# A recurrent cell followed by an MLP: the first group's instructions in a new order, with SyncE's queue and the PSUM banks written out, and a transposition of two steps at once

## The chip, the cores and the metric

The kernel runs on one core of one Trainium2 chip. The metric is the device time of one execution in microseconds (us). Engines are named as in the profile: PE is TensorE, PEld its weight load, DVE is VectorE, ACT is ScalarE, POOL is GpSimd, and SP is SyncE, which here does nothing but issue DMAs.

## The reference, cut to what matters

For each of 32 pairs of batch and head (4 by 8) a recurrence runs over 768 positions with vectors of 40 (abridged):

```python
m_new = np.maximum(f_gate[:, :, t] + m, i_gate[:, :, t])
f_stab = np.exp(f_gate[:, :, t] + m - m_new); i_stab = np.exp(i_gate[:, :, t] - m_new)
C = f_stab * C + i_stab * np.einsum('bhd,bhe->bhde', vt, kt)
n = f_stab * n + i_stab * kt
h = np.einsum('bhde,bhe->bhd', C, qt)
h = C @ qt;  nq = n @ qt          # per batch and head
y[:, :, t] = sigmoid(o_gate[:, :, t]) * h / np.maximum(np.abs(nq), 1.0)
```

The result, arranged as 3072 tokens of 320 numbers, goes through `h = x @ w_in` (320 by 2048), `g = maximum(0.01 h, h)` and `g @ w_out` (2048 by 320). The two weight matrices arrive as 64-bit floats.

## The kernel before, in words

**Steps, chunks and groups.** The 768 positions are cut into six chunks of 128. A *step* is one chunk of one batch, with its eight heads: steps 0 to 3 are chunk 0, steps 4 to 7 chunk 1, and so on. A *group* is the 512 tokens of one chunk in all four batches, and the MLP runs a group at a time. Groups 1 to 5 follow a plan by unit numbers (VISITS, MIXES and so on) which the change leaves alone. The first group is another matter: while its MLP runs, chunk 1 is computed, the weights are still arriving and are brought to 32 bits. Its work is listed by hand in a long string, ORDER, which `first_chunk` reads from left to right and turns into calls. The string fixes the order of the instructions on TensorE, DVE, ACT and POOL (a manual schedule). SyncE's queue is not among them: the tile scheduler places its DMAs.

**Chunk 0** is computed with plain attention. In ORDER, `g`, `ge` and `ug` are the gates of a chunk (`gates` L289, two scans and small operations on DVE; `gates_exp` L319; `gates_T` L341, their transposes on TensorE). `mk` and `ab` (`mask_first` L455, `spread_first` L462) spread them over TensorE, and `exp` (`exp_first`, L475) takes the exponential of two heads on ACT, four times a step. `tr` (`u_transpose`, L584) transposes k and q, `tc` copies the result to SBUF as kqT on ACT or DVE, `sc` (`u_scores`, L599) multiplies q and k, `scm` (`scores_mix`, L610, two per step, DVE) multiplies scores with the exponentials, `val` (`u_values`, L680) multiplies with v, `st` (`state`, L615) and `stc` (L626) make the state behind the chunk, `den` and `gate` (L692) finish the step on DVE, `o` is its output gate on ACT. `x` (`u_x`, L881) transposes the step's result, and `xc` (L890) copies it as xT for the MLP.

**Chunk 1** is computed in halves of 64 positions. `us` (`u_split`, L566) transposes k and q of a step in four quadrants of TensorE, `qs` scales q by its gate, `tq` (`split_qs`, L557) transposes the scaled q of one step, `ex` are the exponentials (L500 on ACT), two heads at a time after a mask on POOL (`pm`, L492), `up` (`u_parts`, L647) makes the scores and the states of the halves, `upl` (`u_plain`, L715) the values, `ux` the transposes of the result, `ug2` the gates of the chunk after it. `fd` loads a step (`load`, L361, and `spread`), `ll` are later loads, `lw` loads a weight tile (L207).

**The MLP of group 0** is 32 units (`ff`, `ff_units` L911). ff 0 to ff 15 each multiply x by two blocks of w_in in products of 256 columns, 20 matmuls at L918, and ACT applies the leaky ReLU (L926). ff 16 to ff 31 multiply by w_out (L953). Units of later groups use L918 with 512 columns.

**Weights.** `narrow_weights` (`nw`, L251) turns a tile of 64-bit weights into 32 bits: one ACT operation (L263) and six on DVE (L265 to L280), which ORDER interleaves one by one with other work. Tiles 0 to 3 are w_in (1280 columns, in two loads each) and tiles 4 to 11 are w_out (640). ff 0, 4, 8 and 12 are the first to need tiles 0, 1, 2 and 3; ff 16 + 4m is the first to need tiles 4 + 2m and 5 + 2m.

**PSUM.** Eight banks: the MLP's products use four (pool `psf`), everything else of the cell the other four (pool `psc`, one tag with four buffers). With the rotating buffers, the fifth allocation waits until the readers of the first are done, in program order.

**Gate inputs.** f and i of chunk 0 (f0 and i0) are each loaded four times, into four groups of 32 partitions, f0 through ACT's queue and i0 through SP's (L93, L94). ACT's queue also issues the gate loads of chunks 1 and 2 (`load_fi`).

Of the kernel before, what the change touches and what calls it, by code (L numbers as in the profile page):

```python
# [22 lines left out]
def kernel(  # L23
# [68 lines left out]
    for r in range(RG):  # L92
        nc.scalar.dma_start(f0[ts(r, BH), :], f_all[:, :P])  # L93
        nc.sync.dma_start(i0[ts(r, BH), :], i_all[:, :P])  # L94
# [266 lines left out]
    def load(s, i=None):  # L361
# [13 lines left out]
        flat = w[:].rearrange("p h t -> p (h t)")
        d["w"] = flat[:, : H * SL].rearrange("p (h t) -> p h t", t=SL)
        if c == 1:
            for u in range(2):
                for i in range(2):
                    nc.sync.dma_start(  # L380
# [57 lines left out]
    def spread(s):  # L438
# [3 lines left out]
        for u in range(2):  # L442
            nc.sync.dma_start(d["w"][ts(u, SL)], a_dr[c, 0, u, b * H : (b + 1) * H, :].partition_broadcast(SL))

    def spread_q(s):
# [111 lines left out]
    def split_qs(s):  # L557

        tq = [psc.tile([P, H, SL], F32, name=f"tq{u}", tag="c") for u in range(2)]
        for h in range(H):  # L560
            for u, toks, rows in subs(s):
                nc.tensor.matmul(tq[u][rows, h, :], lhsT=st[s]["qs"][toks, h], rhs=ident[toks, toks], start=True, stop=True)
# [722 lines left out]
```

## Time and profile before

| what | value |
|---|---|
| three runs, us | 492.03, 491.97, 485.73 |
| median, us | 491.97 |
| time of the profiled execution, us | 488.21 |
| its span, us | 486.4 |
| PE busy in the span | 98% |
| DVE busy | 73% |
| ACT busy | 40% |
| POOL busy | 33% |

The profiled execution is one run of the program with the profiler on. Its span runs from the first to the last recorded instruction, and the execution's own time is 1.8 us more. A row with times in us gives first the start, counted from the start of the span, then the length, then the engine and the instruction with its line. In a row by groups, the number behind the bar is the busy time, then the mean of one instruction in ns, then the idle time of the engine just before the group and what ended it. In a row by windows come the window, its length, then the busy times (with the numbers of instructions) of PE, PE's weight loads, DVE, ACT and POOL, and at the end the granted clock of TensorE as a share of full speed, the mean busy share of the 16 DMA engines and their GB/s.

### The profile page before, as it was taken

What the parts mean: (1) busy time and instruction counts of PE and PEld (TensorE: products, weight loads), DVE (VectorE), ACT (ScalarE), POOL (GpSimd) and SP (SyncE); (2) the same over time, 40 slices, a digit from 0 to 9 for tenths busy, and PEclk for the clock granted to TensorE, in tenths of its full rate; (3) what the DMA queues carried; (4) which work ended last, traced back from release to release, by engine and by line L of the source; (5) the groups of instructions that cost most, each with busy time, mean ns of one, the idle gap of its engine ahead of it and who ended that gap; (6) DMA issues with size and microseconds to landing.
All of it is one profiled execution on the core that took longest, in us unless ns stands there. A gap on an engine that the chain in (4) does not pass through costs nothing.

```text
span 486.4 us, 12790 instructions
## 1 busy us (share of the span) xinstructions
PE 476.2 (98%) x5145; PEld 378.6 (78%) x5145; DVE 357.5 (73%) x581; ACT 194.8 (40%) x509; POOL 158.6 (33%) x207
## 2 busy tenths in 40 slices
PE   8899999899999999999999999999999999999997
PEld 7788887677746489965559985558998899988997
DVE  3887788978926999677898878679899968335611
ACT  3766549554442240414251131425024642156310
POOL 4074342443401816636370654544210002000020
PEclk9979999999999999999999999999999999999999
DMA  8999878775545577776776767754151030100001
GB/s 147 194 206 164 210 180 207 166 167 114 143 138 100 143 158 215 170 179 162 156 190 183 173 156 185 192 135 139 43 230 42 1 108 1 42 16 1 0 1 55
DMA packets 142187, 63.41 MB, mean 130 GB/s; under 512 B 110320, under 2 KB 130352, under 8 KB 142128
## 3 DMA queue, kind: packets, MB, share of 16 engines
q1 hardware_dynamic: 141744, 62.47, 54.3%
q8 instruction: 40, 0.66, 0.5%
q10 hardware_dynamic: 384, 0.13, 0.1%
q14 instruction: 19, 0.16, 0.1%
HBM read 51.68 MB, written 8.27 MB: 123 GB/s over the span
## 4 chain that ended last, share of the span: by engine, by line
PE 90%; DVE 3%; ACT 3%; issue 1%; POOL 1%; POOLq 0%; DVEq 0%
PE po L994 32%; PE ph L918 28%; PE ph L844 8%; PE po L953 5%; PE pe L844 4%; PE pT L754 3%; PE sd L661 3%; PE warm L339 1%; PE pa L684 1%; PE sd L666 1%; ACT w L483 1%; DVE qn L671 1%; PE hN L724 1%; PE tk L576 1%; ACT kqT L582 1%
## 5 line engine op out<-in xcount | busy, mean ns | idle before, releaser
L918 PE MATMUL ph<-xT,w_in 64*128 64x512 f32 (+1 forms) x800 | 144.0, 513 | 0.1
L918 PEld LDWEIGHTS ph<-xT,w_in 64*128 64x128 f32 x800 | 77.9, 190 | 56.7 <-issue 51.3
L994 PE MATMUL po<-w_out,acts 128*128 128x160 f32 x640 | 91.0, 301 | 0.0
L994 PEld LDWEIGHTS po<-w_out,acts 128*128 128x128 f32 x640 | 87.5, 190 | 3.4 <-ACT w L500 1.5
L926 ACT ACTIVATE acts<-ph 128x512 f32<-128x512 f32 (+1 forms) x80 | 37.4, 508 | 89.6 <-PE ph L918 89.1
L641 POOL TENSOR_TENSOR S<-S,f 40x336 f32<-40x336 f32 x36 | 32.5, 903 | 83.4 <-PE pT L754 53.1
L500 ACT ACTIVATE w<-w,gT 128x64 f32<-128x64 f32 x160 | 41.7, 339 | 27.8 <-POOL w L492 27.8
L994 PE MATMUL po<-raw,acts 128*128 128x160 f32 x320 | 45.1, 300 | 0.0
L994 PEld LDWEIGHTS po<-raw,acts 128*128 128x128 f32 x320 | 44.0, 190 | 0.0
L1027 POOL TENSOR_TENSOR y<-y,raw 128x160 f32<-128x160 f32 x10 | 5.5, 555 | 112.0 <-ACT y L1026 112.0
L671 DVE TENSOR_TENSOR qn<-w,sd 64x512 f32<-64x512 f32 x40 | 27.3, 683 | 18.6 <-PE sd L666 12.1
L953 PE MATMUL po<-w_out,acts 128*128 128x320 f32 x128 | 38.2, 454 | 0.0
L866 DVE SCALAR_TENSOR_TENSOR acts<-ph,acts 128x512 f32<-128x512 f32 x32 | 20.6, 685 | 20.6 <-ACT acts L864 20.6
L492 POOL TENSOR_TENSOR w<-w,i 128x512 f32<-128x512 f32 x20 | 32.8, 1644 | 6.9 <-DMA w<-a_dr 3.6
L553 DVE TENSOR_TENSOR qn<-kqT,late 64x512 f32<-64x512 f32 x32 | 34.0, 1062 | 1.0
L953 PEld LDWEIGHTS po<-w_out,acts 128*128 128x128 f32 x128 | 24.7, 198 | 10.0 <-issue 1.2
L768 POOL TENSOR_TENSOR xb<-xb,den 128x320 f32<-128x320 f32 x16 | 11.6, 727 | 48.9 <-DVE xb L765 48.9
L864 ACT ACTIVATE acts<-pe 128x512 f32<-128x512 f32 x32 | 17.4, 594 | 19.1 <-PE pe L844 19.0
L772 DVE STREAM_TRANSPOSE x<-xb 128x512 f32<-128x512 f32 x16 | 17.7, 1107 | 8.0 <-POOL xb L768 8.0
L661 PEld LDWEIGHTS sd<-kqT 40*64 40x64 f32 x640 | 19.6, 135 | 4.6 <-issue 4.2
L870 ACT ACTIVATE acts<-acts 128x512 f32<-128x512 f32 x32 | 19.7, 633 | 8.0 <-DVE acts L866 8.0
L994 PE MATMUL po<-raw 128*128 128x160 f32 x160 | 22.7, 300 | 0.0
(171 smaller groups left out, 768.0 us busy)
## 6 DMA issues: line engine op xcount, KB each, us to landing
w<-a_dr SPq DMA_DIRECT2D x40, 128.0 KB, 3.6
rb<-in_k_dram SPq DMA_DIRECT2D x64, 80.0 KB, 2.7
rb<-in_q_dram SPq DMA_DIRECT2D x64, 80.0 KB, 2.5
rb<-in_o_gate_dram SPq DMA_DIRECT2D x64, 80.0 KB, 2.4
xT<-x_dr SPq DMA_DIRECT2D x32, 160.0 KB, 3.2
late<-a_dr SPq DMA_DIRECT2D x32, 128.0 KB, 3.2
x_dr<-x SPq DMA_DIRECT2D x16, 256.0 KB, 2.8
kn<-in_k_dram SPq DMA_DIRECT2D x24, 160.0 KB, 4.1
```

The lines of the kernel that those rows point to most:

```text
L492: nc.gpsimd.tensor_tensor(w, w, cm2.unsqueeze(1).to_broadcast([P, H, SL]), op=ALU.add)
L500: yield nc.scalar.activation(w[:, h, :], w[:, h, :], AF.Exp, bias=gT[c][:, 0, bh : bh + 1], scale=1.0)
L553: nc.vector.tensor_tensor(mixed(s)[rows, 1 - r], d["kqT"][rows, 1].rearrange("p (h t) -> p h t", t=SL), d["ea"][rows], op=ALU.mult,)
L641: nc.gpsimd.tensor_tensor(new, old, g, op=ALU.mult)
L661: nc.tensor.matmul(bank[1 - u][toks, h, :], lhsT=kqT[rows, 0, ts(h, SL)], rhs=kqT[rows, 1, ts(h, SL)], start=True, stop=True,)
L671: nc.vector.tensor_tensor(mixed(s)[toks, u], w[toks], bank[1 - u][toks], op=ALU.mult)
L844: nc.tensor.matmul(ph[r][:], lhsT=parts["w", key][n][part, at : at + P], rhs=xs[key][part, slot, :], start=start and slot == 0, stop=stop ...
L866: nc.vector.scalar_tensor_tensor(fs[r], in0=ph[r][:], scalar=1.0 + EPS, in1=fs[r], op0=ALU.mult, op1=ALU.add,)
L918: nc.tensor.matmul(ph[r][:, cols], lhsT=w_row(r, slot, j), rhs=xT[DP * r : DP * (r + 1), slot, bs, :], start=(slot == 0), stop=(slot == KC ...
L926: nc.scalar.activation(acts[:, f, cols], ph[r][:, cols], AF.Prelu, alpha=0.01)
L953: nc.tensor.matmul(po[n][:], lhsT=acts[:, f, ts(n, P)], rhs=w_out[:, f, :], start=(f == 0), stop=(f == NF - 1),)
L994: nc.tensor.matmul(bank[:], lhsT=left[:, f, :], rhs=right[:, f, :], start=f == 0, stop=f == KH - 1)
```

## The change

The change does five things, all in the first group.

1. ORDER is written anew. TensorE's pieces of chunk 0 come in another sequence (`sc 0` and `sc 1` back to back, `val` 0 to 3 spread among transposes, scores and states; `x 2` and `st 3` behind ff 0), `us 7` and the `tq` of step 5 stand ahead of ff 16, and the `nw` steps of DVE come in another interleaving.
2. SyncE's queue is in the manual schedule too, so that every load goes out in the order of the string. The loads, `fd` above all, are cut into pieces with names of their own (`fk` for k, `fv` for v, `fs` for the spread gates, `lv` for a w_out tile), and the loads of f0 and i0 (`mf`, `mi`), the memsets (`zk`, `zs`, `zr`), the identities (`id`, `ib`) and the mask (`cm`) become entries of the string as well. The last argument of a load chooses the queue: 1 is ACT's, 0 is SP's. The i0 pieces are now the second, fifth, seventh and ninth DMA of SP; ACT's queue issues only the four of f0.
3. The four buffers of `psc` become four tags of one buffer, and a string of 59 digits, BANKS, says for each allocation of the first group which bank it gets.
4. `split_qs` transposes the scaled q of two steps, s and s + 1, in four quadrants of TensorE; ORDER calls it for steps 4 and 6 in place of four calls for 4, 5, 6 and 7.
5. Behind the first group the PSUM pool is closed, and a pool with four rotating buffers opens in its place for the rest.

The diff, cut to its core (the replacements of `nc.sync` by `queue(on)` and of `psc.tile` by `bank_of` go on in the same way in the other functions):

```diff
-    psc = ctx.enter_context(tc.tile_pool(name="psc", bufs=4, space=PSUM))
+    banks_stack = ctx.enter_context(ExitStack())
+    psc = banks_stack.enter_context(tc.tile_pool(name="psc", bufs=1, space=PSUM))
...
+    banks = []
+    later = []
+
+    def bank_of(shape, name):
+
+        if later:
+            return later[0].tile(shape, F32, name=name, tag="c")
+        return psc.tile(shape, F32, name=name, tag=f"c{banks.pop(0)}")
...
-    for r in range(RG):
-        nc.scalar.dma_start(f0[ts(r, BH), :], f_all[:, :P])
-        nc.sync.dma_start(i0[ts(r, BH), :], i_all[:, :P])
...
+    def queue(on):
+        return nc.scalar if on else nc.sync
+
+    def load_f0(r, on):
+        queue(on).dma_start(f0[ts(r, BH), :], f_all[:, :P])
+
+    def load_i0(r, on):
+        queue(on).dma_start(i0[ts(r, BH), :], i_all[:, :P])
...
+    def load_fi(c, on=0):
         t = fi[c] = wk.tile([BH, 2, P], F32, name="fi")
-        eng = nc.scalar if c < 3 else nc.sync
+        eng = queue(on)
         eng.dma_start(t[:, 0, :], f_all[:, ts(c, P)])
         eng.dma_start(t[:, 1, :], i_all[:, ts(c, P)])
 
-    load_fi(1)
-    load_fi(2)
...
-        tg = psc.tile([P, 5, BH], F32, name="tg", tag="c")
+        tg = bank_of([P, 5, BH], "tg")
...
     def split_qs(s):
 
-        tq = [psc.tile([P, H, SL], F32, name=f"tq{u}", tag="c") for u in range(2)]
+        tq = [bank_of([P, H, SL], f"tq{u}") for u in range(2)]
+        at = [(n, u, toks, rows, rows if n == 0 else slice(SL * u, SL * u + D)) for n in range(2) for u, toks, rows in subs(s)]
         for h in range(H):
-            for u, toks, rows in subs(s):
-                nc.tensor.matmul(tq[u][rows, h, :], lhsT=st[s]["qs"][toks, h], rhs=ident[toks, toks], start=True, stop=True)
-        for u, toks, rows in subs(s):
-            nc.scalar.copy(mixed(s)[rows, u], tq[u][rows])
+            for n, u, toks, rows, to in at:
+                nc.tensor.matmul(tq[u][to, h, :], lhsT=st[s + n]["qs"][toks, h], rhs=ident[toks, toks], start=True, stop=True)
+        for n, u, toks, rows, to in at:
+            nc.scalar.copy(mixed(s + n)[rows, u], tq[u][to])
...
+    BANKS = "01230123030210321031231031021020201320131231012012302320312"
     ORDER = """
-warm 12; g 0; ld 0 0; mk 0; ab 0; ge 0; ld 0 1; ld 1 0; lo 1; ld 0 2; ld 1 1; ld 2 0; ug 0; exp 0 0
-ld 1 2; exp 1 0; exp 1 2; exp 0 2; exp 0 3; tr 0 0; tc 0 0 0; tr 0 1; exp 0 1; tr 1 0; tc 0 1 0
-exp 1 3; ld 2 1; tr 1 1; sc 0; lw 0 0; scm 0 0; lw 0 1; tc 1 0 0; scm 0 1; mk 2; ab 2; lo 0; tc 1 1 0
-ld 3 0; g 1; ld 3 1; ld 3 2; sc 1; exp 1 1; scm 1 1; ld 2 2; exp 2 0; tr 2 0; tr 2 1; tc 2 1 0; lw 1 0
-lw 1 1; vu 0; exp 2 2; val 0; fi 3; exp 3 0; lo 2; exp 3 2; st 0; scm 1 0; stc 0 0 0; exp 2 3
-stc 0 1 0; den 0; exp 2 1; lo 3; tc 2 0 1; sc 2; o 1; lw 2 0; o 0; scm 2 0; gate 0; gp 0; ge 1
-scm 2 1; nw 0; val 1; den 1; x 0; xc 0 1; gate 1; tr 3 0; tr 3 1; tc 3 1 1; nw 0; nw 0; gp 1; x 1
-tc 3 0 0; sc 3; xc 1 1; vu 3; nw 0; nw 0; st 3; vu 2; vu 1; val 2; exp 3 1; exp 3 3; stc 3 1 1; st 2
-stc 2 1 1; scm 3 1; scm 3 0; val 3; nw 0; tiles; ps 3; stc 2 0 1; stc 3 0 1; nw 0; o 2; den 2; den 3
-gate 2; o 3; gate 3; nw 1; st 1; nw 1; nw 1; ug 1; ff 0; gp 2; x 2; xc 2 1; gp 3; nw 1; nw 1; x 3
-xc 3 1; ff 1; nw 1; ff 2; nw 1; ps 0; g 2; lw 2 1; nw 2; ff 3; lw 3 0; lw 3 1; ps 2; ff 4; ff 5; nw 2
-nw 2; ff 6; nw 2; ff 7; fd 4; lw 4; lw 5; stc 1 0 1; ps 1; vu 4; nw 2; nw 2; nw 2; nw 3; nw 3; nw 3
-nw 3; nw 3; nw 3; nw 3; nw 4; ff 8; ff 9; ff 10; nw 4; ff 11; ff 12; nw 4; nw 4; ff 13; nw 4; nw 4
-nw 4; stc 1 1 0; pm 4; sn 4 0; fd 5; ll 5 1; nw 5; ll 4 1; us 4; lw 6; lw 7; fd 6; lz 6; vu 6; fd 7
-qs 5; qs 4; pm 6; us 5; lw 8; nw 5; nw 5; nw 5; nw 5; nw 5; ff 14; pm 5; nw 5; ll 5 2; lw 9; nw 6
-nw 6; lz 7; nw 6; lz 4; ex 4 3; nw 6; ff 15; ll 6 0; ex 4 3; ex 4 2; nw 6; ll 4 2; nw 6; ge 2; nw 6
-pm 7; nw 7; ex 6 3; ex 6 3; tq 4; sn 5 0; nw 7; ll 7 0; ll 7 1; vu 5; up 4; nw 7; ff 16; ff 17; ex 7 3
-ff 18; ff 19; nw 7; ll 8 0; nw 7; nw 7; nw 7; nw 8; nw 8; nw 8; nw 8; ug2 2; nw 8; nw 8; tq 5; upl 4
-lw 10; nw 8; vu 7; ll 6 1; nw 9; nw 9; nw 9; lw 11; lz 5; fd 8; ex 7 3; nw 9; ll 9 0; nw 9; ex 5 3
-nw 9; sn 6 0; nw 9; ex 5 3; ff 20; nw 10; nw 10; qs 6; ex 5 2; up 5; us 7; qs 7; nw 10; nw 10; ff 21
-sn 7 0; ff 22; ux 4; upl 5; ll 9 1; nw 10; nw 10; nw 10; nw 11; nw 11; nw 11; ex 6 2; ff 23; pv 8
-sq 9; nw 11; ll 7 2; nw 11; tq 7; us 6; ll 8 1; pm 8; lz 8; ex 8 3; tq 6; ff 24; nw 11; nw 11; xb0
-ll 6 2; up 6; ex 7 2; up 7; ff 25; upl 6; fd 9; sn 9 0; upl 7; kq 9; fd 10; pv 9; sq 8; ll 8 2; pm 9
-kq 8; ll 11 1; sq 11; fd 11; ll 10 1; sn 8 0; ll 9 2; ex 8 3; ll 11 0; lz 9; vu 8; vu 9; ff 26; ff 27
-ff 28; ff 29; ux 5; ux 6; ux 7; sq 10; ff 30; ex 8 2; ff 31; ex 9 3; ex 9 3; ll 10 0; ex 9 2
+mf 3 1; ld 0 2 0; mi 1 0; mf 2 1; id; ld 0 0 0; cm; ld 1 1 0; mi 2 0; ib; ld 0 1 0; zk 1; mi 3 0
+mf 1 1; ld 1 0 0; mi 0 0; zr; warm 12; mf 0 1; zk 0; mk 0; zk 2; zk 3; lw 0 0 0; lw 0 1 0; zs 2; zs 3
+g 0; ge 0; ug 0; ab 0; exp 0 0; exp 1 0; exp 0 2; tiles; zs 1; ld 1 2 0; tr 0 0; tc 0 0 0; tr 0 1
+tr 1 0; tr 1 1; tc 1 1 1; tc 0 1 0; sc 0; exp 1 2; exp 1 3; fi 1 0; exp 1 1; tc 1 0 0; sc 1; scm 1 0
+scm 1 1; exp 0 3; mk 2; exp 0 1; scm 0 1; nw 0; scm 0 0; ld 2 0 0; lo 0 0; ab 2; zs 0; vu 0; g 1; o 0
+val 0; nw 0; nw 0; tr 2 0; ld 2 1 0; tr 2 1; nw 0; exp 3 0; exp 3 1; exp 2 0; exp 2 3; lo 1 0; val 1
+den 0; ld 3 0 0; tr 3 0; tc 2 0 1; gate 0; o 1; tc 2 1 1; lo 3 0; gp 0; sc 2; exp 2 1; ld 3 1 0; den 1
+tc 3 0 1; gate 1; gp 1; vu 1; tr 3 1; exp 2 2; scm 2 0; ps 0; x 0; scm 2 1; nw 0; tc 3 1 1; ld 2 2 0
+vu 2; ld 3 2 0; exp 3 2; sc 3; lw 1 0 0; exp 3 3; scm 3 0; scm 3 1; lo 2 0; vu 3; val 2; ge 1; x 1
+st 0; val 3; st 2; nw 0; ps 2; xc 0 1; lw 1 1 0; xc 1 1; nw 0; fi 2 0; o 3; st 1; stc 1 0 0; gate 3
+stc 0 1 1; fk 4 0; stc 0 0 1; o 2; den 3; gp 3; gate 2; ff 0; den 2; lw 2 0 0; gp 2; lw 2 1 0
+stc 1 1 1; ll 4 1 0; ug 1; fs 4 0; x 3; lw 3 0 0; lw 3 1 0; st 3; stc 3 0 1; xc 3 0; ll 6 0 0; fk 7 0
+lz 7; nw 1; nw 1; nw 1; nw 1; nw 1; pm 4; x 2; nw 1; nw 1; xc 2 1; vu 4; fk 5 0; lz 5; fs 5 0; ff 1
+ff 2; ff 3; nw 2; nw 2; nw 2; lz 4; nw 2; nw 2; stc 3 1 0; lv 5 0; nw 2; nw 2; lv 4 0; ll 5 1 0; us 4
+stc 2 0 1; fk 6 0; stc 2 1 0; ff 4; ff 5; ff 6; ff 7; nw 3; nw 3; nw 3; nw 3; nw 3; nw 3; ll 4 2 0
+fs 7 0; ff 8; nw 3; qs 4; ps 1; ff 9; ff 10; ex 4 3; qs 5; vu 6; nw 4; lv 6 0; nw 5; nw 5; ll 6 1 0
+ff 11; ps 3; pm 5; lv 7 0; nw 5; tq 4; lv 8 0; us 5; fv 4 0; ff 12; ll 7 1 0; nw 5; ex 4 2; fv 5 0
+ll 5 2 0; sn 4 0; nw 5; nw 5; fs 6 0; fv 6 0; ll 7 0 0; nw 4; ff 13; g 2; ff 14; sn 7 0; lv 9 0; lz 6
+nw 5; nw 4; nw 4; nw 4; nw 4; nw 4; nw 6; nw 6; nw 6; fi 3 0; ge 2; sq 9 0; fk 8 0; nw 6; ex 4 3
+ff 15; up 4; us 7; lz 8; nw 6; sn 5 0; ex 5 3; ex 5 3; ff 16; nw 6; lv 11 0; nw 6; sn 6 0; qs 7; nw 7
+nw 7; nw 7; vu 5; fk 9 0; nw 7; nw 7; lz 9; lv 10 0; ff 17; ff 18; nw 7; nw 7; ex 5 2; upl 4; ff 19
+pm 6; nw 9; nw 9; nw 9; ll 6 2 0; pm 7; ex 6 2; nw 9; nw 9; up 5; nw 9; nw 8; us 6; fk 10 0; nw 8
+ex 6 3; nw 8; nw 8; nw 8; ll 8 0 0; ff 20; ff 21; ux 4; upl 5; ll 7 2 0; ex 6 3; vu 7; nw 9; ff 22
+nw 8; nw 8; ll 9 1 0; fv 7 0; nw 10; sq 8 0; qs 6; ll 8 1 0; fs 9 0; ff 23; up 6; nw 10; nw 10; nw 10
+nw 10; nw 10; ex 7 3; tq 6; ff 24; ll 9 0 0; nw 10; ff 25; nw 11; ux 5; xb0; ug2 2; sn 9 0; fs 8 0
+upl 6; ll 8 2 0; ex 7 3; ex 7 2; up 7; fv 8 0; ff 26; ff 27; fv 10 0; ux 6; nw 11; nw 11; nw 11; nw 11
+nw 11; fk 11 0; fv 9 0; fs 11 0; pm 9; nw 11; upl 7; ll 9 2 0; ff 28; ff 29; ex 9 2; kq 8; ll 10 0 0
+ff 30; ux 7; fv 11 0; ff 31; vu 8; ex 9 3; ex 9 3; vu 9; sq 10 0; pv 9; pv 8; sn 8 0; pm 8; ex 8 3
+kq 9; ll 11 0 0; ex 8 3; fs 10 0; ll 10 1 0; ex 8 2; ll 11 1 0; sq 11 0
...
+        banks.extend(map(int, BANKS))
...
-            "warmer": warmer, "idle": idle, "fd": feed, "ll": load_late,
+            "warmer": warmer, "idle": idle, "fk": lambda s, on: load(s, 0, on), "fv": lambda s, on: load(s, 1, on), "fs": spread, "ll": load_late,
...
     with tc.manual_schedule(engines={E.PE, E.DVE, E.Activation, E.Pool}):
-        first_chunk()
+        with tc.manual_schedule(engines={E.SP}):
+            first_chunk()
+        banks_stack.close()
+        later.append(ctx.enter_context(tc.tile_pool(name="psl", bufs=4, space=PSUM)))
```

More of the change, by code (lines that the diff above doesn't have):

```diff
@@ L570, in u_split @@
         src = (d["k"], natural(s, 1))
-        bank = [psc.tile([P, H, SL], F32, name=f"tk{r}", tag="c") for r in range(2)]
+        bank = [bank_of([P, H, SL], f"tk{r}") for r in range(2)]
         for h in range(H):
@@ L601, in u_scores @@
         kqT = d["kqT"]
-        sc = d["sc"] = [psc.tile([P, PR, P], F32, name=f"sc{r}", tag="c") for r in range(2)]
+        sc = d["sc"] = [bank_of([P, PR, P], f"sc{r}") for r in range(2)]
         for j in range(PR):
@@ L651, in u_parts @@
         run(lazy.pop(s))
-        bank = [psc.tile([P, H, SL], F32, name=f"sd{r}", tag="c") for r in range(2)]
+        bank = [bank_of([P, H, SL], f"sd{r}") for r in range(2)]
         ends = 2 if c + 1 < NB else 1
@@ L859, in third @@
             def third():
[L860 removed]
+                pe.extend(bank_of([P, GT], f"pe{r}") for r in range(2))
                 rows(j, pe, "dif", True, True)
```

95 lines of the change are left out of this document (51 added, 44 removed).

## The prediction

> **What bounds the kernel now.** I read the page's busy shares first, then the stages, then the chain of work that ended last, in order of time.
>
> ```profile
> PE 476.2 (98%) x5145; PEld 378.6 (78%) x5145; DVE 357.5 (73%) x581; ACT 194.8 (40%) x509; POOL 158.6 (33%) x207
> ```
>
> ```profile
> 9.68 3.98 ACT w L483 x15
> ...
> 15.44 1.09 PE sc L606 x16
> ...
> 17.56 1.90 PE pa L684 x16
> ...
> 35.32 3.84 PE ph L918 x20
> ...
> 69.27 1.97 PE tk L576 x128
> ...
> 88.70 1.14 PE hN L724 x32
> ...
> 93.93 1.72 issue
> ...
> 102.37 0.22 PE xt L887 x2
> ...
> 106.11 0.96 PE tq L562 x30
> ...
> 111.89 0.17 PE sd L661
> ...
> 113.81 0.20 PE sd L666
> ...
> 119.07 8.81 PE po L953 x32
> ...
> 133.17 13.08 PE ph L918 x60
> ...
> 483.26 0.32 DVE y L1051
> ```
>
> Columns: start, length, what. From 119 us on the chain is TensorE piece after piece; the first group ends at 133.2 and the 353.2 us behind it (486.4 - 133.2) are TensorE work that the edit does not touch. So only the first 133.2 us can change, and a microsecond there is a microsecond of the whole, if the vector-engine tail of the group is done in time.
>
> TensorE's need from the first FF unit (35.3 us, `ff 0`) to the end of the group, from these rows: 32 units at 2.2 (8.81 for four) 70.4; the transposes of x 2 and x 3, 0.7; `us` 4 at 1.0 (1.97 for two) 4.0; `tq` 4 at 0.96, 3.8; `up` 4 at 1.0 (111.89 to 114.01 for two) 4.0; `upl` 4 at 1.1, 4.4; `ux` 4 at 0.33 (0.22 and a third transpose), 1.3; `ug2` 0.7. Sum 89.3, so 124.6 would do; 133.2 was needed. That is 8.6 us lost, and part of it is the clock:
>
> ```profile
> 31.60:38.50 6.90, 6.90 (x47) 6.11 (x49) 6.44 (x15) 1.92 (x3) 4.04 (x8) 0.52 1.07 215
> 94.00:96.00 2.00, 0.35 (x19) 0.35 (x18) 1.97 (x3) 0.00 (x0) 1.84 (x3) 1.00 0.06 11
> 96.00:100.00 4.00, 4.00 (x18) 2.64 (x10) 3.91 (x6) 2.32 (x4) 2.92 (x3) 0.57 0.56 139
> ```
>
> The granted clock, the figure behind the five engines' busy times, is 0.52 from 31.6 to 38.5 (half of the 3.2 us behind 35.3 lost, 1.6) and 0.57 from 96 to 100, after TensorE's pause of 1.72 us at 93.9 (1.7 of the four lost): 3.3. The other 5.3 us are waits for DVE and ACT.
>
> **The change, part by part.** I follow the new order engine by engine with these durations:
>
> ```profile
> 4.42 0.40 DVE L302 TENSOR_TENSOR_SCAN m<-f,i 128x128 f32<-128x128 f32 x1
> ...
> 15.06 0.40 DVE L296 TENSOR_TENSOR_SCAN F<-fi,zeros 32x128 f32<-32x128 f32 x1
> ...
> 16.67 0.14 DVE L316 TENSOR_TENSOR na<-m,F 32x1 f32<-32x1 f32 x1
> ```
>
> ```profile
> 35.74 0.49 DVE L265 TENSOR_SCALAR late<-late 128x1280 bf16<-128x1280 bf16 x1 [0.26 <-ACT late L263]
> ...
> 41.18 1.49 DVE L280 SCALAR_TENSOR_TENSOR w_in<-w_in,late 128x1280 f32<-128x1280 f32 x1
> ```
>
> ```profile
> L671 DVE TENSOR_TENSOR qn<-w,sd 64x512 f32<-64x512 f32 x8 | 5.5, 684 | 0.1
> L613 DVE TENSOR_TENSOR w<-w,sc 128x512 f32<-128x512 f32 x8 | 5.3, 673 | 2.4 <-ACT w L483 2.4
> ```
>
> ```profile
> 76.79 0.34 DVE L265 TENSOR_SCALAR xb<-xb 128x640 bf16<-128x640 bf16 x1 [1.52 <-ACT xb L263]
> ...
> 80.59 0.82 DVE L280 SCALAR_TENSOR_TENSOR w_out<-w_out,xb 128x640 f32<-128x640 f32 x1
> ...
> 110.74 0.33 DVE L267 TENSOR_SCALAR late<-late 128x640 uint16<-128x640 uint16 x1
> ...
> 113.23 0.82 DVE L280 SCALAR_TENSOR_TENSOR w_out<-w_out,late 128x640 f32<-128x640 f32 x1
> ```
>
> ```profile
> L582 ACT COPY kqT<-tk 40x512 f32<-40x512 f32 x16 | 9.3, 579 | 2.6 <-PE tk L576 2.3
> L900 ACT COPY xT<-xt 64x384 f32<-64x384 f32 x16 | 7.5, 471 | 5.2 <-PE xt L888 5.1
> L263 ACT ACTIVATE late<-raw 128x1280 bf16<-128x1280 bf16 x2 | 2.7, 1354 | 0.0
> L500 ACT ACTIVATE w<-w,gT 128x64 f32<-128x64 f32 x38 | 10.1, 339 | 0.0
> ```
>
> So: gates of a chunk 1.75 us; a w_in tile (`nw` 0 to 3) 6.9 on DVE after 1.35 on ACT; a w_out tile (`nw` 4 to 11) 4.6 on DVE (76.79 to 81.41; undisturbed 3.6: five of the six in 3.3 at 110.74), after 0.8 on ACT (a half-width tile).
>
> *Gate inputs.* The four pieces of i0 were SP's first four DMAs; now they are its second, fifth, seventh and ninth, behind v, k and q. Before, the scan over f and i began at 4.42.
>
> ```profile
> 0.74 1.79 SPq L94 DMA_DIRECT2D i<-in_i_gate_dram  x4
> ```
>
> ```profile
> i<-in_i_gate_dram SPq DMA_DIRECT2D x4, 16.0 KB, 1.7
> S<-in_v_dram SPq DMA_DIRECT2D x4, 160.0 KB, 3.3
> raw<-in_moe_w_in_dram SPq DMA_DIRECT2D x4, 640.0 KB, 11.6
> acts<-in_moe_w_in_dram SPq DMA_DIRECT2D x4, 640.0 KB, 8.0
> ```
>
> The sixth DMA waits until the first has landed (0.7 + 3.3 = 4.0), the ninth goes out near 5.6 and lands 1.7 to 4.4 us later. I take 2.1, so 7.7. The exponentials (L483), at 9.7 before, come no sooner than 11.2, since both gate transposes now stand ahead of the spreading matmuls: +1.5.
>
> *Chunk 0 up to ff 0.* ACT's 16 exponentials (3.98 for 15) and one kqT copy (0.67) between them end at 16.1. DVE: the four products of steps 0 and 1 with the scores (0.67 each, from the end of `sc 1` at 15.4 on) until 18.1, the gates of chunk 1 until 19.8, three operations of `nw 0` (2.9) until 22.7, then denominator and gate of step 0 until 24.0, of step 1 until 25.2. TensorE: `val 0` (1.9) from 18.1, two transposes, `val 1`, `tr 3 0` until 23.4. From here the banks decide. `sc 2` goes into the bank of step 0's values and waits for gate 0: 24.0 to 25.1. `tr 3 1` goes into that of step 1 and waits for gate 1: 25.2 to 25.8, its copy on ACT ends at 26.5, `sc 3` (1.1) at 27.6, `val 2` at 29.5, x 1 at 29.9, `st 0` at 30.4, `val 3` at 32.3, `st 2` at 32.8. ACT: from 26.5 four exponentials and the gates' four until 28.6, eight copies of x 0 and x 1 (0.42 each by the xT row and its shorter half) until 32.0, a tanh and step 0's two state copies until 33.1. `st 1` takes the bank of that state: 33.1 to 33.6. `nw 0` is done by 31.9, so ff 0 starts at 33.6, against 35.3. Gain 1.7; `ug 1` and `st 3` (1.2 of TensorE) move behind ff 0, which takes most of it back. A handover between engines is counted at nothing here; a tenth of a microsecond in each of ten would cost 1.
>
> *ff 1 to ff 15.* x 2's copies on ACT let ff 2 start at 40.8 (0.8 of wait); `nw 1` runs 39.2 to 46.1, just when `us 4` ends (46.2), so ff 4 starts then. ACT's first step of `nw 2` and `nw 3` stands behind the ReLU of ff 3 and ff 7; they end at 54.6 and 64.0, ahead of ff 8 (55.0) and ff 12 (65.8). ff 14 waits 0.8 for ACT, which has eight copies (4.6 us) of `tq` and `us 5` ahead of ff 12's ReLU. ff 15 ends at 75.4, `up 4` and `us 7` at 77.4.
>
> ```profile
> 77.59 8.88 PE L953 MATMUL po<-w_out,acts 128*128 128x320 f32 x32
> ```
>
> Before, ff 16 began at 77.6, without `us 7` and without step 5's `tq`: 2.2 us ahead in all.
>
> *The paired tq.* A pair issues as many matmuls as a `us`, in the same four quadrants: 1.0 for two steps, not 1.9. Two pairs save 1.9 of TensorE (bounds 0, if the quadrants don't overlap, and 1.9; the `tk` row is the same shape, so 1.9). ACT's copies stay eight.
>
> *ff 16 to ff 31.* DVE carries, beside the w_out tiles, 1.9 us a step behind `up` (two products of 0.68 and a state addition of half a microsecond) and 1.7 behind `upl` (denominators and gate as in chunk 0, 1.2, and another addition). From `nw 3`'s end at 64.0 and 0.8 of ACT: `nw 5`, the gates of chunk 2 and `nw 4`, 11.0, until 75.8; 0.8 of ACT, `nw 6` with step 4's 1.9 inside, until 83.4. ACT reaches `nw 7` only after the ReLU of ff 15 (79.6), four copies (2.3) and six exponentials (2.0), at 83.9, so DVE ends it at 89.3 (0.8 + 4.6) and step 4's 1.7 at 91.0. TensorE has done ff 16 to 19, `upl 4` and `up 5` at 88.3, and `us 6` takes the bank of step 4's last state: a new wait of 2.7. Behind `us 6` on TensorE stand ff 20 and all that follows. `nw 9` and 8 are ready at 103.9 (91.0 + 9.2 + 1.9 + 1.7), ff 24 wants them at 104.2. `nw 10` ends at 110.4, `nw 11`, behind steps 6 and 7, at 119.0: ff 28, at 117.6, waits 1.4. From there four units and `ux 7`, 9.1: 128.1.
>
> *SP in a fixed order.* Before, its queue stood longest at one place, v of step 4:
>
> ```profile
> 34.70 11.67 SPq L380 DMA_DIRECT2D S<-in_v_dram  x4
> ```
>
> Now k of step 4 waits for `st 0` (30.4), and behind it stand w_in tile 2, q of step 4, its spread and w_in tile 3. Tile 2 lands by 42.0 (11.6 after), needed at 46.0; tile 3 goes out five DMAs later and is needed at 55.8. I cost SP at nothing; 4.0 us of slack cover it, and beyond that each microsecond counts.
>
> *At nothing:* the moved memsets (POOL and DVE idle before 9 us), the four gate loads fewer on ACT, the change of PSUM pool at the end (its first user is the fifth unit of group 1, behind 11 us of solid TensorE).
>
> Sum: 128.1, plus 1.0 for a slow clock (0 if it stays full, 3.3 as before; the waits of 2.7 and 1.4 hide part of one) is 129.1, or 4.1 less than 133.2. The profiled execution took 488.2 (span 486.4): 488.2 - 4.1 = 484.1. The median shown, 492.0, is 3.8 above it, the lowest run 2.5 below; about 2% is what a measurement of this kernel can tell from no change, 482.1 and 501.8 around that median.
>
> **Rivals.**
>
> 1. *TensorE stays fed.* The w_out tiles take the undisturbed 3.6: four of them ahead of `us 6` give 4.0 back, more than its wait; ff 28 doesn't wait and no slow clock comes. 128.1 - 2.7 - 1.4 = 124.0, 9.2 less: 479.0. For it: DVE has fewer waits for ACT; against: POOL keeps disturbing DVE. On the clock, the Trainium skill ("TensorE: Matmul & The Clock Gate", "What's actually happening") says that half rate follows a whole idle window of about 3.4 us; by that rule no wait above brings it, and the sum would be 483.1. The trace differs: a pause of 1.72 us was followed by 0.57.
>
> 2. *The start is late.* The last piece of i0 is served like the w_in halves near it (8.0, not 2.1): exponentials and ff 0 slip 4 to 5 us, 488.4. For it: the DMA share (last but one figure) is 1.07 from 31.6 to 38.5, so queues are full early; against: the piece is issued ahead of w_in.
>
> 3. *SP holds, and it gets slower.* Place: k of step 4. If it is held 11.67 us as step 4's v was, it goes out at 42.1, w_in tile 2 lands at 53.7, 7.7 late, `nw 2`, `nw 3` and ff 8 with it: 129.1 + 7.7 = 136.8, 491.8; a hold twice that gives 503. It decides from `st 0` at 34.4 on; against it: nothing in the walk delays `st 0` so.
>
> **How the numbers follow.** Forecast 0.58 (own range 481 to 487), rival 1 0.20, rival 2 0.12, rival 3 0.10. The range 478.5 to 491.5 leaves out the faster part of rival 1 and most of rival 3's tail. Faster by over 2%: rival 1 and 0.06 of the forecast's edge, 0.26. Slower by over 2%: half of rival 3, 0.05. Within 2%: 0.69.
>
> **What would show it.** ff 0's first `ph` near 33.6 (over 36: rival 2); L483 from 11.2; ff 4 near 46.2; two `tq` groups of about 1.0 us, 64 matmul records each; a pause before `us 6` near 88 (none: rival 1); the first `ph` of 512 columns of group 1 near 129; the clock rows behind 90 us. It is wrong if the group's end moves and the time does not, or if the stretch behind it changes length by over 1 us.

## The result, and the profile after

In 20 runs each the changed kernel took 483.03 us (median; 480.59 to 486.44) and the kernel before 488.98 (485.73 to 494.69). The ratio is 0.9887, with a 95% interval of 0.9862 to 0.9912: 1.1% faster, which is within 2%. The forecast was 484.1. In each ratio, here and below, runs over 1.5% above the fastest of the same kernel beside them are left out; medians are of all runs.

The profiled execution of the changed kernel took 486.44 us, the longest of its 20 runs; its span is 484.7 us. That alone says that one profile is not the kernel. Each run also reports its mean granted clock, and the times go by it: the six runs with a clock of 0.999 to 1.000 took 480.6 to 482.0, the eight with 0.996 took 482.7 to 483.5, the four with 0.993 took 484.1 to 485.5, the two with 0.989 took 485.6 and 486.4. So the view to read first is the clock. The first fence has windows of that profile, the second three of the same windows of a second profile of the changed kernel (481.01 us, clock 1.000, experiment e1). The columns are the window, its length, the busy time and number of instructions of PE, PEld, DVE, ACT and POOL, the granted clock, the DMA share and GB/s.

```profile
24.30:27.70 3.40, 3.05 (x35) 2.66 (x33) 3.18 (x5) 3.08 (x11) 2.64 (x6) 1.00 1.17 196
27.70:31.10 3.40, 3.40 (x31) 2.93 (x30) 2.98 (x3) 2.69 (x8) 0.98 (x1) 0.53 1.04 192
31.10:34.50 3.40, 3.40 (x42) 3.32 (x43) 0.00 (x0) 1.47 (x4) 0.49 (x3) 0.50 1.11 194
34.50:38.00 3.50, 3.50 (x26) 2.81 (x24) 2.39 (x9) 0.00 (x0) 2.90 (x7) 0.50 1.05 206
38.00:41.40 3.40, 3.40 (x41) 2.54 (x39) 1.66 (x5) 1.80 (x5) 0.34 (x1) 0.98 1.20 183
```

```profile
27.70:31.10 3.40, 3.11 (x39) 2.74 (x38) 2.78 (x2) 3.25 (x9) 2.05 (x2) 1.00 1.11 205
31.10:34.50 3.40, 3.17 (x53) 2.61 (x54) 2.06 (x8) 0.71 (x2) 2.50 (x7) 1.00 1.16 197
34.50:38.00 3.50, 3.50 (x44) 2.88 (x45) 2.75 (x9) 2.72 (x6) 1.02 (x2) 1.00 1.06 209
```

The same work, and in the first profile 10.2 us of it (27.9 to 38.1, behind a window at full clock) run at half clock: 5.1 us lost, which is the whole difference between the two spans (484.7 and 479.2) but 0.4. The chain of waits of the first profile shows where it goes:

```profile
34.81 4.01 PE ph L946 x20
...
40.86 1.37 ACT late L287
42.26 0.50 DVE late L289
...
48.58 1.91 DVE w_in L304
...
50.62 8.93 PE ph L946 x80
...
69.08 1.50 DVE w_in L304
...
76.10 0.58 ACT kqT L610
76.71 0.39 ACT acts L954
77.14 4.86 PE ph L946 x39
...
83.97 6.66 PE po L981 x24
...
131.48 13.08 PE ph L946 x60
...
481.53 0.32 DVE y L1079
```

The new order's chain runs through VectorE and ScalarE once the start is late: ff 4 waits for tile 1 of w_in (until 50.6), ff 12 for tile 3, ff 14 for ScalarE, which has eight copies of 0.58 ahead of a ReLU. From ff 16 (84.0) on it is TensorE piece after piece, and group 1 begins at 131.4 (L946 with 512 columns). What follows is 353.2 us, as before.

### The profile page after: what moved, and what is told of

It is laid out like the page before. It is cut to its first block, busy times and chain, and to the rows that moved or that the text cites. A ratio compares the mean times of both kernels' runs of the same rounds, so it can differ in the third digit from the quotient of the medians.

```text
span 484.7 us, 12784 instructions
## 1 busy us (share of the span) xinstructions
PE 473.7 (98%) x5145; PEld 378.7 (78%) x5145; DVE 358.1 (74%) x582; ACT 194.6 (40%) x508; POOL 157.3 (32%) x207
## 4 chain that ended last, share of the span: by engine, by line
PE 90%; DVE 4%; ACT 3%; DMA 1%; issue 1%; SPq 0%; DVEq 0%
PE po L1022 32%; PE ph L946 25%; PE ph L872 8%; PE po L981 7%; PE pe L872 4%; PE pT L782 3%; PE sd L689 3%; PE pa L712 2%; PE sd L694 1%; DVE w_in L302 1%; DVE late L293 1%; PE tkq L618 1%; DVE w_in L304 1%; PE hN L752 1%; DVE w_in L298 1%
## 5 line engine op out<-in xcount | busy, mean ns | idle before, releaser
L946 PE MATMUL ph<-xT,w_in 64*128 64x512 f32 (+1 forms) x800 | 144.5, 513 | 4.0 <-DVE w_in L304 2.1
L946 PEld LDWEIGHTS ph<-xT,w_in 64*128 64x128 f32 x800 | 80.3, 190 | 58.5 <-issue 51.8
L669 POOL TENSOR_TENSOR S<-S,f 40x336 f32<-40x336 f32 x36 | 34.2, 953 | 70.4 <-PE pT L782 46.6
L981 PE MATMUL po<-w_out,acts 128*128 128x320 f32 x128 | 36.5, 438 | 0.0
L519 POOL TENSOR_TENSOR w<-w,i 128x512 f32<-128x512 f32 x20 | 31.8, 1592 | 6.6 <-ACT acts L954 6.0
L892 ACT ACTIVATE acts<-pe 128x512 f32<-128x512 f32 x32 | 17.4, 595 | 18.9 <-PE pe L872 18.9
```

Source lines behind the costliest of these rows:

```text
L519: nc.gpsimd.tensor_tensor(w, w, cm2.unsqueeze(1).to_broadcast([P, H, SL]), op=ALU.add)
L669: nc.gpsimd.tensor_tensor(new, old, g, op=ALU.mult)
L946: nc.tensor.matmul(ph[r][:, cols], lhsT=w_row(r, slot, j), rhs=xT[DP * r : DP * (r + 1), slot, bs, :], start=(slot == 0), stop=(slot == KC ...
L981: nc.tensor.matmul(po[n][:], lhsT=acts[:, f, ts(n, P)], rhs=w_out[:, f, :], start=(f == 0), stop=(f == NF - 1),)
```

## The experiments

"At an equal clock" below compares runs with the same mean granted clock. The runs of both kernels for which the clock is on record, 98 of before and 32 of the changed one, give the reference. The table has medians; 16 runs of before and one of the changed kernel, at clocks that have no row, are left out of it, but not of the sums below.

| mean granted clock | before, us (runs) | changed, us (runs) |
|---|---|---|
| 1.000 | 483.7 (1) | 481.3 (9) |
| 0.996 | 486.6 (2) | 483.2 (10) |
| 0.993 | 486.6 (14) | 485.3 (9) |
| 0.989 | 487.4 (20) | 486.0 (2) |
| 0.986 and 0.985 | 489.2 (24) | 487.0 (1) |
| 0.979 | 492.0 (21) | none |

**e0 and e1: both kernels again, for the clock of each run.** No edit.

> The kernel before, unchanged, to see the granted clock of each of its runs. Theory A (clock): part of the gain is that the new order meets fewer stretches of half clock; each stretch is 3.41 us long and loses 1.7, so the runs lie near 483 + 1.7 x n with n mostly 2 to 5 (mean granted clock 0.993 to 0.982), and hardly any run has a clock of 1.000. Theory B (work): the order of the work alone is worth the 5.5 us of the medians; then runs of the kernel before with a clock of 0.996 to 1.000 exist and take 486 or more.

> The changed kernel, unchanged, for a second profile. Theory A: the group ends at 126.3 + 1.7 x n with n stretches of half clock, the rest stays at 353.2; median 483. Theory B: the group's end does not follow the clock. Both: ff 4 waits 1 to 2 us for tile 1 of w_in and ff 14 for ScalarE's copies, as in the first profile (1.50 and 1.83), because both waits stand in the order.

Measured: before 489.65 (12 runs), 1.0042 (1.0001 to 1.0084) of the runs of the same kernel beside it, so that medians here can't tell less than half a per cent; changed 484.0 (12 runs; ratio 0.9926, 0.9888 to 0.9963), with its group 1 beginning at 126.0 at full clock, where 126.3 was expected:

```profile
125.97 1.56 PE L946 MATMUL ph<-xT,w_in 64*128 64x512 f32 x6
```

A straight line through each kernel's runs, against the time lost to the clock (1 less the mean clock, times the span), gives 483.6 + 0.81 per us lost for the kernel before, whose mean loss is 6.8, and 481.4 + 0.94 per us for the changed one, whose mean loss is 2.1. Of the 5.7 between the two means, 2.2 are the order of the work and 3.5 (0.81 x 6.8 less 0.94 x 2.1) are clock. Theory A holds in kind, and the size of its clock part is new: the larger half of the gain. The line of the kernel before is carried out to a loss that hardly any of its runs has, and its end there is uncertain by about a quarter of a microsecond; at a clock of 1.000, 483.7 (one run) and 481.3 agree with the 2.2. Why the new order meets fewer stretches of half clock is not shown, and no run has the new order of the engines alone, so that the 2.2 are known only by the pieces that are taken out below. Only three of the 98 runs of the kernel before have a clock of 0.996 or more, and one of them (487.5; the others 485.7 and 483.7) takes the 486 of theory B; it lies 2.4 above the line, by a cause that no profile here shows. The waits expected in the second profile were not there: ff 4 didn't wait, and ff 14 waited 0.75 instead of 1.83.

**e2: the pair serial.** The 64 matmuls of a pair, in the order of two single calls:

```diff
-        for h in range(H):
-            for n, u, toks, rows, to in at:
+        for m, h in [(m, h) for m in range(2) for h in range(H)]:
+            for n, u, toks, rows, to in at[2 * m : 2 * m + 2]:
```

> The changed kernel with the paired transposition issued step by step (the same 64 matmuls, banks and copies, two quadrants at a time). If four quadrants overlap as priced, each of the two groups takes 2.0 us instead of 1.1, and the time rises by 1.0 to 1.9 (one of the two may lie in a wait). Rival: quadrants do not matter to the time, below 0.5.

Measured: 485.49 (twelve runs, one of them 695.29 at a clock of 0.651; ratio to before 0.9961, 0.9923 to 0.9998), and 481.9, 482.0 and 482.4 at a clock of 1.000, against 481.3. The second pair, in the profile of e1 and then of e2, both at full clock:

```profile
101.87 1.10 PE L590 MATMUL tq<-ident,y 64*40 64x64 f32 x64 [0.94 <-POOL y L556]
```

```profile
102.06 1.80 PE L590 MATMUL tq<-ident,y 64*40 64x64 f32 x64 [0.95 <-POOL y L556]
```

The four quadrants do overlap, and save 0.7 here. Group 1 began at 126.0 and 126.9, of which 0.2 lay ahead of this pair. The first pair saves the same on TensorE, but ff 14 behind it then waits less for ScalarE (0.75 gone), so it brings nearly nothing. The pairs are worth 0.7 to 0.9, not 1.9.

**e3: rotating PSUM buffers instead of the banks written out.**

```diff
-    psc = banks_stack.enter_context(tc.tile_pool(name="psc", bufs=1, space=PSUM))
+    psc = banks_stack.enter_context(tc.tile_pool(name="psc", bufs=4, space=PSUM))
...
-        if later:
-            return later[0].tile(shape, F32, name=name, tag="c")
-        return psc.tile(shape, F32, name=name, tag=f"c{banks.pop(0)}")
+        return (later[0] if later else psc).tile(shape, F32, name=name, tag="c")
```

> The changed kernel with four rotating PSUM buffers instead of the banks written out, the order unchanged. If the banks matter: new waits on TensorE of 1 to 4 us in all (sc 2, tr 3 1, us and up wait for another bank than before), time up by 1 to 5. Rival: the banks written out bring nothing by themselves, within 1 us.

Measured: 485.34 (twelve runs, mean clock 0.9915; ratio 0.9948, 0.9911 to 0.9985), where e1 had 484.0 at a mean clock of 0.9952. At an equal clock little is left of this 1.3: 481.7 at 1.000 (one run) and 483.4 to 484.0 at 0.996 (four), some 0.4 above the changed kernel. The rival holds at an equal clock: the 59 digits are worth about half a microsecond. Whether they also raise the clock, twelve runs can't tell.

**e4: SyncE's queue left to the scheduler.**

```diff
-        with tc.manual_schedule(engines={E.SP}):
-            first_chunk()
+        first_chunk()
```

> The changed kernel with SyncE's queue left to the tile scheduler, all else as in the change. The prediction priced SyncE's order at nothing: then the group ends within 1 us of 126.0 at a clock of 1.000, the time is within 1 of the changed kernel's 481.2. Rival: the order of the loads brings something; then the exponentials begin later or a weight tile lands late, and it is 1 to 4 us slower at an equal clock.

Measured: 496.57 us, ratio to before 1.0156 (1.0110 to 1.0202), 13 above the changed kernel's median. At a like clock less is left: 9 to 11 above the one changed run there (495.8 to 497.9 at 0.983 and 0.985, against 487.0), and 7.6 above the changed kernel's line from e1. It is slower than the kernel before, and further off than even the rival's 1 to 4. The longest wait of TensorE says why (us in all, times, longest); the next two rows are of SyncE's queue, in e4 and in e1:

```profile
PE tk L604 <- DMA rb<-in_q_dram: 12.8, 1, 12.8
```

```profile
91.31 0.40 SPq L441 DMA_DIRECT2D rb<-in_q_dram  x1
```

```profile
66.19 2.74 SPq L441 DMA_DIRECT2D rb<-in_q_dram  x1
```

`us 7` stands ahead of ff 16 in the new order, and its q is a load that the scheduler sends at 91.3 and the string by 69. All of ff 16 to 31 waits behind it, and the clock falls in the wait. The theory under test, that the order of the loads is worth nothing, fell.

**e9: SyncE's queue in the order of the string, in the kernel before.** The same line added to the kernel before.

> The kernel before with SyncE's queue put in the manual schedule too, in the order in which its own string names the loads; order of the engines, banks and transpositions as before. Theory: the string of the kernel before was not written for SyncE; what the changed kernel needs is its own order of loads (left to the scheduler it lost 13 us), not a fixed order as such, so this is no faster than before at an equal clock, within 1 us or slower. Rival: a fixed order of the loads is worth something by itself, 1 to 3 us faster at an equal clock.

Measured: 485.57, where the 17 runs beside it had 488.92; ratio 0.9976 (0.9940 to 1.0012), the same within 2%. Part of the difference of the medians is clock (mean 0.9896 and 0.9864): at 0.993 it took 484.6 to 486.8 (five runs; before 484.4 to 487.0), at 0.989 485.6, 485.6 and 488.5 (before 486.1 to 488.7). Against the line of the kernel before it is 0.9 faster, and by the interval between 0.6 slower and 2.9 faster, so the rival's 1 to 3 is neither shown nor out. A fixed order as such is not where the 13 of e4 come from.

**e7: the pair alone, in the kernel before.** The new `split_qs` with its two banks; "tq 5" and "tq 7" struck from ORDER.

> The kernel before with the paired transposition alone (tq 4 makes 4 and 5, tq 6 makes 6 and 7; the calls tq 5 and tq 7 are gone, order, queues and banks as before). From the serial experiment (0.9 at clock 1.000) and the price of the prediction (1.9 in all, part of it in waits for DVE): 0.8 to 1.9 less at an equal clock, around 487.5 to 488. Rival: the four calls lie in front of waits for DVE in this order, and the pair brings nothing (within 0.5).

Measured: 487.78, ratio 1.0003 (0.9968 to 1.0039), that is from 1.6 us faster to 1.9 slower. No gain is seen, but the interval is too wide to part the rival (within 0.5) from a gain of 0.8, and against the line of the kernel before the runs are 0.6 faster. The profile speaks for the rival: what TensorE no longer does it now largely waits. Its two waits for VectorE ahead of hN, 0.52 and 0.59 in the profile of before, are here:

```profile
PE hN L725 <- DVE qn L672: 2.1, 1, 2.1
PE hN L725 <- DVE S L646: 0.9, 1, 0.9
```

**e5, e6 and e8: idle matmuls in chunk 0.** They write into banks which the real products overwrite (arguments shortened); e5 in the changed kernel, e6 in the kernel before, e8 in the kernel before with narrow ones.

```diff
+    def fill(flat, cols, n):                      # e5, e6: bf16, wide
+        for _ in range(n):
+            nc.tensor.matmul(flat[:, :cols], lhsT=ident_b[:], rhs=repeated(ident_b, cols), start=True, stop=True)
...
+        fill(sc[0], 4 * P, 1)                     # in u_scores; e8: 3 of 41 columns, f32
...
+        fill(pa, 2 * P, 3)                        # in u_values; e8: 4 of 41 columns, f32
```

> The changed kernel with idle matmuls of full width in chunk 0: one of 128x512 (bf16, identity by identity) into the score bank ahead of each of sc 0 to 3, three of 128x256 into the bank of val 0 to 3, overwritten by the real products. They do no work of the reference. Cost by the 128x512 product of the mask (0.3 us): at most 4 x 0.3 + 12 x 0.15 = 3.0 on TensorE, part of it in waits. Theory A1 (the clock falls because chunk 0's products are narrow): the runs have a clock of 1.000 nearly always, the spread of the times shrinks from 6 us to 2, the median is 481.2 + 1 to 3. Theory A2 (the half clock is drawn by something else): the same mixture of clocks as before (4 of 12 at 1.000), median 485 to 487.

> The kernel before with the same idle matmuls. Theory A1: the clock goes from about 0.986 to 0.996 or more, and the median falls from 489 to 485 to 487 although TensorE has up to 3 us more to do: most of what the change gained is had without it. Theory A2: clocks as before, time 489 to 492.

> The kernel before with idle matmuls at the same places as in the filled one (e6), of about the same TensorE time, but narrow: three products of 41 columns (f32) into the score bank of each step of chunk 0, four into the bank of its values (0.12 us each, 3.3 in all against 3.5). They do no work of the reference. Theory A1 (narrow products do not hold the clock): the granted clock stays near 0.986, the half-rate stretches stay in chunk 0, and the time rises to about 490 to 491. Rival A3 (the filled waits did it, not the width): clock 0.995 as in e6, time 487 to 488.

Measured: e6 487.76 (ratio 0.9979, 0.9951 to 1.0008), its mean clock 0.9957, where the kernel before had 0.9873 in the runs beside it. e5 483.6 (0.9890, 0.9847 to 0.9933), clock 0.9975. e8 496.81 (1.0165, 1.0123 to 1.0206), clock 0.9828. The windows of e6 (first) and of e8, in chunk 0 and behind it:

```profile
24.30:27.70 3.40, 2.27 (x35) 1.67 (x36) 3.37 (x5) 3.29 (x9) 3.40 (x4) 1.00 1.07 211
27.70:31.10 3.40, 3.40 (x54) 3.21 (x48) 2.79 (x4) 1.75 (x8) 3.34 (x6) 1.00 1.29 188
31.10:34.50 3.40, 3.40 (x43) 3.19 (x44) 3.23 (x10) 1.80 (x5) 1.74 (x6) 1.00 1.05 209
```

```profile
31.10:34.50 3.40, 3.40 (x51) 3.25 (x45) 2.96 (x4) 1.01 (x4) 3.34 (x6) 1.00 0.96 190
34.50:38.00 3.50, 3.50 (x20) 3.50 (x18) 1.96 (x5) 2.85 (x6) 0.77 (x4) 0.53 1.09 213
38.00:41.40 3.40, 3.40 (x31) 3.24 (x30) 1.62 (x6) 0.00 (x0) 1.13 (x3) 0.50 1.06 207
41.40:45.00 3.60, 3.60 (x18) 2.93 (x19) 3.57 (x7) 0.00 (x0) 3.33 (x8) 0.51 1.14 201
```

In e6 TensorE is idle for a third of the window from 24.3 (2.27 of 3.40) and the clock holds; in e8 it is busy throughout from 31.1, with narrow products, and the clock falls. The narrow fill was dearer than we had priced (8.2 us busy, not 3.3: its 28 products in f32 are 56 records of some 0.3 us each), so the time is 496.8 and not the expected 490 to 491, and it still didn't hold the clock. So it is not the filled waits (A3 falls): the wide fill raised the clock and the narrow one did not, as A1 has it. But the wide products are bf16 and the narrow ones f32, and no run has wide f32 or narrow bf16: that the width, or the count of streamed columns, is what matters, and not the type, is argued, not shown. In the changed kernel the fill shows less: three of the six runs of e5 have a clock of 1.000, where "nearly always" was expected and e1 has four of twelve, and the times spread over 3.9, not 2. Its profile has no half clock from 14 to 45 us, but one stretch at 10.4 and one at 75.3, behind pauses of TensorE of 1.4 and 1.8. In time, e6 gave what the clock saved (0.0084 of some 485 us, 4.1) back to the 3.5 us for which its fill keeps TensorE busy: the expected 485 to 487 was missed by a microsecond.

**e10 and e11: a better version.** e10 takes ScalarE's first step of three tiles out from behind ReLUs; e11 adds a light fill. The lines of ORDER are cut at their ends.

```diff
-ff 4; ff 5; ff 6; ff 7; nw 3; nw 3; nw 3; nw 3; nw 3; nw 3; ll 4 2 0
+ff 4; ff 5; nw 3; ff 6; ff 7; nw 3; nw 3; nw 3; nw 3; nw 3; ll 4 2 0
...
-ff 9; ff 10; ex 4 3; qs 5; vu 6; nw 4; lv 6 0; nw 5; nw 5;
+ff 9; nw 4; nw 5; ff 10; ex 4 3; qs 5; vu 6; lv 6 0; nw 5;
```

> The changed kernel with ScalarE's first step of tile 3 moved ahead of ff 6 (it stood behind ff 7's ReLU), and those of tiles 4 and 5 ahead of ff 10; nothing else. VectorE stood idle for 2 to 4 us ahead of tile 3, so it ends tile 3 and all later tiles 2 to 3 us earlier. If its tiles still hold TensorE (the waits of 0.6 ahead of ff 12, 0.75 to 1.8 ahead of ff 14): 0.7 to 2 us less, 479.5 to 480.5 at a clock of 1.000. Rival: at full clock TensorE is the only bound by then, and the time is the same within 0.5.

> e10 with a few idle matmuls against the half clock: twelve of 128x128 (bf16) into the bank of the first gates, where TensorE waits 1.1 to 1.8 us, two of 128x256 into the bank of val 1 to 3, one of 128x512 into that of sc 2 and 3. They do no work of the reference. Theory A1: no half-rate stretch in chunk 0, clock 0.998 or more, cost 0.5 to 1 on TensorE; the median falls to 481 to 482, under the changed kernel's 483 to 484. Theory A2: clock and spread as in e10, and about 1 us slower than e10 at an equal clock.

Measured: e10 480.17 (0.9828, 0.9787 to 0.9870), 479.7 and 480.0 at a clock of 1.000, 1.5 below the changed kernel there. e11 479.55 (0.9820, 0.9776 to 0.9865), its clock 0.9992, four of its six runs within 0.06 of each other. Tile 3 in the first profile of the changed kernel, and in e10's:

```profile
61.46 1.35 DVE L289 TENSOR_SCALAR late<-late 128x1280 bf16<-128x1280 bf16 x1 [4.00 <-ACT late L287]
```

```profile
54.94 0.49 DVE L289 TENSOR_SCALAR late<-late 128x1280 bf16<-128x1280 bf16 x1
```

The idle 4.0 us of VectorE are gone; in e1, at full clock, they were 2.17:

```profile
55.60 0.49 DVE L289 TENSOR_SCALAR late<-late 128x1280 bf16<-128x1280 bf16 x1 [2.17 <-ACT late L287]
```

Both beat both kernels, the changed one also at an equal clock; e11, expected at 481 to 482, came out lower. Its fill costs nothing that can be seen (479.5 at a clock of 1.000, e10 479.8), for twelve of its matmuls stand ahead of a wait of 2 us for the first gates, and the rest lie partly in chunk 0's short ones.

## Why the prediction was right, point by point

The total (484.1 against 483.0) and its sign came out right, and in part by luck: two errors cancel. At full clock the walk ended at 128.1 and the profile of e1 at 126.0: 2.1 too long. For the half clock it added 1.0, and the mean loss is 2.1: 1.1 too short. With the 353.2 behind it, which was right, the two leave the time a microsecond off. Inside the 2.1 two more errors hide, which stand below with the waits ahead of `us 6` and ff 28.

- *Gate inputs:* the last i0 landed at 8.07 in the first profile and 7.86 in e1 (7.7 forecast), the exponentials began at 10.87 and 10.66 (11.2). Right in kind, rival 2 is out.
- *Chunk 0:* ff 0 at 32.1 at full clock, against 33.6. Two thirds of the difference were there before any of the bank waits: the scores of steps 0 and 1 were done at 14.6, not 15.4, `val 0` started at 17.4, not 18.1, and `tr 3 0` ended at 22.4, not 23.4. The forecast then let `sc 2`, `tr 3 1` and `st 1` wait for their banks one after the other; `sc 2` waited 0.21 instead of 0.6. The longest wait in e1 between 17 us and ff 0 is 0.53, and not for a bank:

```profile
31.33 0.81 PE L649 MATMUL dC<-vu,kn 128*40 128x42 f32 x32 [0.53 <-POOL vu L541]
```

- *ff 16:* 76.2 at full clock, against 77.4: the same 1.2 to 1.5, carried on. ff 14's wait was forecast at 0.8 and is 0.75. In the first profile ff 16 began at 84.0.
- *The wait ahead of `us 6`, 2.7, and that ahead of ff 28, 1.4:* neither came. In e1 the waits at `us 6` are 0.32 and 0.17, behind a tile 7 that ended at 86.5:

```profile
85.71 0.82 DVE L304 SCALAR_TENSOR_TENSOR w_out<-w_out,late 128x640 f32<-128x640 f32 x1
```

```profile
87.77 0.27 PE L604 MATMUL tk<-ident,kn 64*40 64x64 f32 x2 [0.32 <-DVE x L763]
88.22 0.25 PE L604 MATMUL tk<-ident,kn 64*40 64x64 f32 x1 [0.17 <-DVE S L673]
```

ScalarE reached tile 7 at 81.6 instead of 83.9, VectorE ended it at 86.5, not 89.3, and the state of step 4 at 88.2, not 91.0. This is the step that failed: VectorE's tiles were booked 1.4 to 2.8 us late through the whole second half (tiles 10 and 11 ended at 108.0 and 117.0, forecast 110.4 and 119.0); up to 1.2 of that is the earlier start of ff 16. The forecast had 50.7 us from ff 16 to the group's end, 4.1 of them these waits, and e1 49.8, with waits of 0.32, 0.17 and one of 0.94 ahead of the second pair that the forecast didn't have (the row of e2). So the pieces of TensorE took some 48.4 us and were booked at 46.6: `us 6` 1.4 for 1.0, `up` 1.15 to 1.3 for 1.0, a unit 2.24 to 2.4 for 2.2. That these 1.8 and the 0.94 hid most of the waits that didn't come is luck. On the two waits rival 1 was right; its 479.0 also needed undisturbed tiles and no half clock, and the changed kernel reached 480.6 at best.
- *The paired tq:* 1.9 forecast, 0.7 to 0.9 measured (e2), and nothing that the medians show in the old order (e7). The matmuls' overlap was right; what was mis-sized is how much of it lay on the path.
- *SyncE at nothing:* nearly right for this order, since no load held TensorE directly in e1. It is not off the chain, though: from 39 to 62, 68 to 77 and 78 to 83 us the chain of waits of e1 is SyncE's queue and three loads that it sends, and from there it goes on over VectorE and POOL towards the 0.94 ahead of the second pair.

```profile
43.15 6.33 SPq L470
```

```profile
57.52 4.28 DMA w<-a_dr
```

The cover that the sum named, 4.0 us, was not what carried it: with another order of the loads 12.8 us of wait appear at `us 7` (e4). Rival 3 named the right kind of loss at another load.
- *The banks:* priced as four waits; by e3 the choice of banks is worth about half a microsecond at an equal clock.
- *The clock:* "1.0 for a slow clock, 3.3 as before". The profile of before had lost 5.1 in the group (3.3 behind ff 0), its runs lose 6.8 on average, the changed kernel's 2.1. The forecast set a gain of 2.3 here and the runs show 3.5. That a whole idle window is needed for half clock, the rule cited from the Trainium skill ("TensorE: Matmul & The Clock Gate", "What's actually happening"), is not what these runs show: stretches began at 31.4 (before), 27.9 (after) and 34.7 (e8) with no pause over 0.4 us in the 3.4 us ahead. One of those in e4 fits the rule: it began at 84.8, inside the wait of 12.8. The free-running window of 3413 ns that the same section gives agrees with their lengths: 10.24 us of half clock in the profile after, and 6.83 and 3.41 in the one before, are three, two and one of it.

## What to carry to other kernels

Read the granted clock of every run before comparing two kernels: here more than half of a gain of 1.1% was clock, and the one profile was the longest run of twenty. Orders of several queues that were found together are one thing: taken apart, one piece was worth 13 us in the medians (SyncE's, without which the new order loses), others a microsecond or less. And what is removed from TensorE counts only where it doesn't stand ahead of a wait for another engine.

## What the hardware showed that we had not expected

The clock falls to one half in stretches of 3.41 us or a multiple of it, each losing 1.7, and where they begin differs from run to run of the same program (31.4 and 96.2 in the profile of before, 22.6 and 29.4 in that of e0). They begin behind a stretch in which TensorE was half idle, as in e4, where the second row follows the first at once:

```profile
6.30:9.70 3.40, 1.59 (x13) 0.74 (x15) 0.97 (x4) 0.40 (x1) 0.47 (x2) 1.00 0.90 190
9.70:13.10 3.40, 3.40 (x40) 3.18 (x40) 0.59 (x2) 1.41 (x6) 2.85 (x8) 0.50 1.06 208
```

They also begin where the records show it busy throughout, with f32 products of 41 and 42 columns (31.4 in before, 34.7 in e8). Some 2.8 us of wide idle matmuls (e11: 0.8 at the gates, 1.2 ahead of the values, 0.8 ahead of the scores) went with a mean clock of 0.9992, where e10 without them had 0.9965; with six runs of each, that is a hint and not a proof. The stronger case is e6: 0.9957 in twelve runs, 0.9873 in the 23 of the kernel before beside it.
